# Linear attention and an expert layer on one core: another order of the instructions in chunks 2 to 8

## The chip, the cores and the metric

The kernel runs on one core of a Trainium2 chip. The metric is the device time of one execution in microseconds, lower being better. A core has engines that work side by side and wait for each other through semaphores: TensorE (PE in the rows, with PEld for its weight loads), VectorE (DVE), ScalarE (ACT), GpSimd (POOL), and SyncE (SP), which here issues the DMAs. Each engine takes its own instructions strictly in order.

## The reference

There are 8 batches of 8 heads with 576 rows of 64. The attention is linear, and its output feeds a two-layer block:

```python
q_s = exp(q - max(q, over the 64)); q_s /= sum + 1e-9
k_s = exp(k - max(k, over the 576 rows)); k_s /= sum + 1e-9
kv  = einsum('bhsd,bhse->bhde', k_s, v)        # 64 x 64 per head
x   = einsum('bhsd,bhde->bhse', q_s, kv)       # heads side by side: 4608 x 512
h   = x @ w_in                                 # 512 -> 2048
out = (h - tanh(h)) @ w_out                    # 2048 -> 512
```

## The kernel before

The 4608 rows of x go in nine chunks of 512. Chunks 0 to 7 are 512 rows of batches 0 to 7; the last 64 rows of all eight batches make chunk 8. The hidden layer goes in 16 blocks of 128 for each chunk. A matrix is held as a high part and a low part, and a product is made as three products of parts.

For each block n of a chunk the steps are these (functions in `h_parts`, lines 654 to 717, and `o_mm`, line 730). `pha`, `phb`, `phc` are four matmuls each into one PSUM tile `ph`. On ScalarE `u`, `t`, `m` (the tile mk) read `ph`, and `vv` reads u. On VectorE `g` and `tt` read `ph` and one tile in SBUF; `gg` and `cp` read SBUF alone. `gh` (ScalarE) and `gl` are the high and low part of g; gl runs on GpSimd or, with a star, on VectorE. `po n.t a` are two matmuls with gh and `po n.t b` is one with gl, for each of four row blocks t, summed over the 16 blocks. PSUM has two tiles `ph`, so `pha` of block n waits until all readers of block n-2 are done; gh, gl, g, t and u have two buffers each, mk and vv one. The second layer lags the first by two blocks.

While a chunk j is in this loop, the words with a + prepare chunk j+1. For q, in two halves 0 and 1: load `q`, maximum `mq`, subtraction `qu`, exponential `qe`, sum `sq`, scaling `qn`, transpose `tb` and a way through DRAM `qp`, `qg`. For k: load `k`, maximum `km` and on to the row of maxima `mrow` (through DRAM: `kp`, `kg`), then for the two full tiles 0 and 1 and for the remainder of 64 rows (tile `kr`, number 2) the subtraction `ks`, the exponential `ke` and the products with v, `pk`. `vo` sets the ones beside v (MEMSET on GpSimd) before `v` is loaded; v has one buffer, so `vo.1` waits for the matmuls `pk.0`. `px` makes x, `xh` and `xl` are its parts. k and v are prepared for chunks 0 to 7 alone: while chunk 7 runs, chunk 8's q is prepared and no k, and while chunk 8 runs, nothing is.

The order on every engine is written out by hand as text: FIRST (lines 32 to 101) for chunks 0 and 1, ROUND (lines 103 to 129) repeated for chunks 2 to 8, LAST for the last blocks. `run` (line 909) calls the word's function, and each engine gets its instructions in the order of the words. `go` (line 890) sends `qu`, `qn`, `gl`, `ks` to GpSimd unless the word ends with a star, which sends it to VectorE.

Of the kernel before, what the change touches and what calls it, by code (L numbers as in the profile page):

```python
# [100 lines left out]
"""  # L101

ROUND = """
ph0 po14.0a u0 po14.0b po14.1a m0 +q.0 pha1 phb1 +vo.2 +mq.0 po14.3a po15.0a po14.1b po14.3b phc1
po14.2a vv0 po14.2b t0 t1 g0 po15.2a gg0 po15.0b tt0 po15.2b cp0 u1 +vo.0 +qu.0 pha2 g1 gh0
po15.1a po15.3a phb2 +qe.0 tt1 po15.1b phc2 pha3 oc.2 po0.0a m1 oc.0 vv1 +sq.0 gg1 po15.3b u2 t2
cp1 phb3 tt2 gl0 os.2 po0.0b po0.2a po0.1a phc3 oc.3 gh1 po1.0a m2 vv2 oc.1 po0.2b g2 t3 u3 m3 gl1
po1.2a gg2 cp2 os.1 tt3 pha4 po0.3a phb4 phc4 +sa.0 os.3 +sr.0 os.0 +qn.0 vv3 po0.1b gh2 pha5 g3
po0.3b po1.1a +k.2 +tb.0 t4 gl2 po1.3a gg3 po1.0b +k.0 cp3 po1.2b u4 tt4 vv4 po2.0a po1.1b g4 gh3
po1.3b m4 po2.0b +k.1 +again +km.a po2.3a phb5 gl3* phc5 po3.0a +km.b gg4 pha6 po2.3b cp4 u5 t5  # L110
phb6 po3.3a +km.c m5 vv5 g5 +qn.1 po2.1a tt5 po3.3b +km.d po2.2a gg5 po2.2b phc6 pha7 phb7 po2.1b
cp5 gh4 po3.0b po3.1a po3.2a t6 gl4 po3.2b +qp.0 +tb.1 +kb po4.0a u6 vv6 +kr m6 +kq.1 gh5 po4.2a
phc7 po4.0b +q.1 gl5 +kq.3 po4.2b +kq.2 po5.0a po3.1b po4.3a po5.2a pha8 tt6 u7 +qp.1 g6 t7 po4.1a
gg6 +kx vv7 +kt po4.1b po5.2b po5.1a m7 phb8 phc8 cp6 +vo.1 g7 po4.3b gg7 tt7 t8 po5.3a +kp po5.0b
po5.3b po5.1b +mq.1 +v.2 +qu.1* gh6 u8 cp7 +v.0 pha9 m8 po6.0a +qg.1 phb9 gl6* gh7 tt8 g8 +kg
+ks.0* po6.1a vv8 phc9 u9 t9 gg8 +qe.1 gl7* po6.0b po7.0a po6.3a +sq.1 tt9 po6.2a +ke.0 +v.1
po6.3b po6.2b cp8 pha10 phb10 vv9 phc10 gh8 po6.1b u10 po7.3a g9 po7.0b po7.1a +sa.1 t10 po7.3b
po8.0a m9 po7.2a +pk.0 +sr.1 pha11 po7.2b po8.3a phb11 vv10 po7.1b gg9 phc11 +qn.3* cp9 +ks.2
po8.2a gl8* po8.0b pha12 phb12 m10 t11 g10 po8.1a +qn.2 +tb.3 gg10 gh9 +ks.1 gl9 u11 po9.0a phc12
po8.1b tt10 +ke.1 +qg.0 +ke.2 +pk.1 vv11 tt11 m11 u12 cp10 +pk.2 t12 po8.3b pha13 g11 po9.3a  # L120
po8.2b po9.0b gg11 cp11 +sl gh10 m12 gl10 +rs phb13 po10.0a +qp.3 +rc +tb.2 po9.2a phc13 vv12
po9.1a u13 po9.2b +qp.2 po9.1b g12 gh11 m13 tt12 +kn vv13 po9.3b po10.0b gg12 t13 po10.3a cp12
+qg.2 po10.1a po10.3b gl11 po10.2a gh12 pha14 po11.0a +px.0 +xh.0.0 g13 po10.2b +qg.3 po10.1b
phb14 gg13 tt13 +xh.0.1 phc14 po11.2a ph15 po11.2b po11.3a gl12 u14 vv14 +xl.0.0 cp13 +xl.0.1
po11.1a g14 po11.1b t14 m14 u15 po11.3b po11.0b po12.0a t15 gg14 po12.0b +px.1 po12.1a po12.2a
po12.3a gh13 tt14 cp14 tt15 gl13* po12.1b po12.3b vv15 po12.2b +xh.1.0 +sv po13.0a g15 po13.2a m15
po13.3a gh14 gg15 +xl.1.0 cp15 +xh.1.1 po13.0b gl14* po13.3b po13.2b po13.1a gh15 po13.1b +xl.1.1
gl15*
"""

LAST = """
# [841 lines left out]
```

## Time and profile before

| | us |
|---|---|
| median of 3 runs | 880.32 (880.26 to 880.8) |
| the profiled execution, its own time | 880.32 |
| its span | 878.5 |
| PE busy | 847.1 (96%) |
| DVE busy | 659.7 (75%) |
| ACT busy | 540.9 (62%) |
| POOL busy | 206.9 (24%) |

The share of busy time says which engine the span is made of; which wait costs time is seen only from the idle time of that engine, by stretch, and from what ended it. In the chain that ended last PE has 83% of the span and DVE 9%. The granted clock (PEclk) is 9 tenths or more in all 40 slices.

### The profile page before, as it was taken

The page shows a single profiled execution, that of the slowest core. Times are in us where ns is not written, and L with a number is a line of the kernel's source. Part 1 is how long each engine was busy: PE and PEld are TensorE (multiplying, and loading weights), DVE is VectorE, ACT ScalarE, POOL GpSimd, SP SyncE. Part 2 cuts the span into 40 slices and gives each one's busy share as a digit, 9 for nine tenths or more (in the row PEclk, how much of TensorE's full clock was granted, in tenths as well). Part 3 has the DMA queues.
Part 4 walks back from the last instruction along what each step waited for, and adds up shares of the span by engine and source line. Part 5 has one row for each costly group of instructions (what it writes and reads, how often), then busy time and mean ns, then how long its engine had stood idle before and what let it go on. Part 6 is the DMA issues. An engine that isn't in the chain of part 4 may idle for free.

```text
span 878.5 us, 13026 instructions
## 1 busy us (share of the span) xinstructions
PE 847.1 (96%) x4810; PEld 693.3 (79%) x4810; DVE 659.7 (75%) x1011; ACT 540.9 (62%) x955; POOL 206.9 (24%) x182
## 2 busy tenths in 40 slices
PE   2999999999999999999999999999999999999997
PEld 2888888878887888878887888788877888888885
DVE  7999989886788658866787668875796667755554
ACT  4999998565655556555665565655555565556553
POOL 4634122221312122221213121212222121201120
PEclk9999999999999999999999999999999999999999
DMA  9975301233331204320332133120422022101002
GB/s 309 362 231 205 109 1 37 84 105 89 113 91 49 67 13 138 79 71 20 115 90 72 43 115 90 49 67 37 124 69 84 20 98 58 47 4 49 1 0 49
DMA packets 103199, 75.83 MB, mean 86 GB/s; under 512 B 17376, under 2 KB 91104, under 8 KB 103136
## 3 DMA queue, kind: packets, MB, share of 16 engines
q1 hardware_dynamic: 103136, 75.01, 27.6%
q8 instruction: 38, 0.62, 0.3%
q14 instruction: 25, 0.20, 0.1%
HBM read 56.10 MB, written 18.89 MB: 85 GB/s over the span
## 4 chain that ended last, share of the span: by engine, by line
PE 83%; DVE 9%; ACT 4%; DMA 1%; issue 1%; SPq 0%; ACTq 0%
PE po L738 39%; PE ph L674 39%; DVE g L687 3%; PE px L631 2%; PE pk L417 1%; DVE t L684 1%; ACT mk L664 1%; DVE g L692 1%; DVE sq L518 1%; ACT t L664 1%; DVE g L679 1%; ACT u L664 1%; DMA k<-in_k_dram 1%; ACT q L513 1%; ACT gh L695 1%
## 5 line engine op out<-in xcount | busy, mean ns | idle before, releaser
L738 PE MATMUL po<-w_o,gh 128*128 128x512 f32 x1152 | 327.7, 391 | 0.0
L674 PE MATMUL ph<-xh,w_i 128*128 128x512 f32 x1152 | 307.0, 391 | 7.5 <-DVE t L684 7.5
L674 PEld LDWEIGHTS ph<-xh,w_i 128*128 128x128 f32 x1152 | 214.9, 188 | 55.3 <-DVE t L684 10.3
L738 PEld LDWEIGHTS po<-w_o,gh 128*128 128x128 f32 x1152 | 215.3, 188 | 45.9 <-issue 1.0
L699 POOL TENSOR_TENSOR gl<-g,gh 128x512 fp32r<-128x512 f32 x80 | 107.0, 1337 | 395.3 <-PE po L738 170.6
L738 PE MATMUL po<-w_o,gl 128*128 128x512 f32 x576 | 194.2, 392 | 0.0
L679 DVE SCALAR_TENSOR_TENSOR g<-u,ph 128x512 f32<-128x512 f32 x144 | 98.3, 683 | 100.2 <-POOL gl L699 35.4
L664 ACT ACTIVATE u<-ph 128x512 f32<-128x512 f32 x144 | 86.1, 598 | 111.5 <-PE ph L674 111.4
L674 PE MATMUL ph<-xl,w_i 128*128 128x512 f32 x576 | 154.2, 389 | 0.0
L664 ACT ACTIVATE t<-ph 128x512 f32<-128x512 f32 x144 | 85.8, 596 | 92.1 <-PE ph L674 91.7
L687 DVE SCALAR_TENSOR_TENSOR g<-vv,g 128x512 f32<-128x512 f32 x144 | 119.8, 832 | 10.5 <-ACT vv L664 6.2
L674 PEld LDWEIGHTS ph<-xl,w_i 128*128 128x128 f32 x576 | 108.1, 188 | 22.9
L738 PEld LDWEIGHTS po<-w_o,gl 128*128 128x128 f32 x576 | 107.6, 188 | 23.5 <-issue 1.2
L695 ACT CAST gh<-g 128x512 fp32r<-128x512 f32 x144 | 89.4, 621 | 59.6 <-PE po L738 43.9
L692 DVE COPY_PREDICATED g<-mk,t 128x512 f32<-128x512 int32 x144 | 120.2, 835 | 7.1 <-ACT mk L664 2.9
L684 DVE TENSOR_TENSOR t<-ph,t 128x512 f32<-128x512 f32 x144 | 98.3, 685 | 33.8 <-ACT mk L664 19.2
L664 ACT ACTIVATE vv<-u,b_pa 128x512 f32<-128x512 f32 x144 | 104.4, 725 | 6.4 <-DVE g L687 3.9
L664 ACT ACTIVATE mk<-ph 128x512 int32<-128x512 f32 x144 | 86.1, 598 | 21.4 <-DVE g L692 9.4
L699 DVE TENSOR_TENSOR gl<-g,gh 128x512 fp32r<-128x512 f32 x64 | 44.6, 697 | 20.7 <-ACT gh L695 17.1
L510 POOL TENSOR_TENSOR q<-q,mq 128x1024 f32<-128x1024 f32 x9 | 18.3, 2032 | 63.8 <-DVE mq L505 63.7
L650 ACT CAST xh<-px 128x512 fp32r<-128x512 f32 x36 | 20.4, 593 | 18.5 <-PE px L631 18.5
L652 DVE TENSOR_TENSOR xl<-px,xh 128x512 fp32r<-128x512 f32 x36 | 24.4, 686 | 7.7 <-ACT xh L650 7.1
(107 smaller groups left out, 529.6 us busy)
## 6 DMA issues: line engine op xcount, KB each, us to landing
k<-in_k_dram SPq DMA_DIRECT2D x16, 512.0 KB, 5.5
raw_i<-in_moe_w_in_dram SPq DMA_DIRECT2D x16, 512.0 KB, 7.0
raw_o<-in_moe_w_out_dram SPq DMA_DIRECT2D x16, 512.0 KB, 7.3
q<-in_q_dram SPq DMA_DIRECT2D x15, 512.0 KB, 4.3
v<-in_v_dram SPq DMA_DIRECT2D x14, 512.0 KB, 4.7
qd<-tb SPq DMA_DIRECT2D x28, 256.0 KB, 2.3
qs<-qd SPq DMA_DIRECT2D x112, 64.0 KB, 2.0
out_dram<-o SPq DMA_DIRECT2D x28, 256.0 KB, 2.2
```

Of the source, the lines that this page charges most:

```text
L510: eng.tensor_tensor(qf, qf, mq, op=ALU.subtract)
L650: nc.scalar.copy(xh, px_of[i][g])
L652: nc.vector.tensor_tensor(xl, px_of[i][g], xh.bitcast(F32), op=ALU.subtract)
L664: nc.scalar.activation(new(tag, **of), st[src], fn, **kw)
L674: nc.tensor.matmul(st["ph"], w[:, i, c], xs[j][x][:, c, :], start=n == 0, stop=n == 3 * NC - 1)
L679: nc.vector.scalar_tensor_tensor(new("g"), st["u"], C2, st["ph"], op0=ALU.mult, op1=ALU.mult)
L684: nc.vector.tensor_tensor(st["t"], st["ph"], st["t"], op=ALU.subtract)
L687: nc.vector.scalar_tensor_tensor(st["g"], st["vv"], PB, st["g"], op0=ALU.add, op1=ALU.mult)
L692: nc.vector.copy_predicated(st["g"], st["mk"], st["t"])
L695: nc.scalar.copy(new("gh", F32R), st["g"])
L699: eng.tensor_tensor(new("gl", F32R), st["g"], st["gh"].bitcast(F32), op=ALU.subtract)
L738: nc.tensor.matmul(po[key], gs[j, f][g][:, cols], wt["o", f][:, w], start=n == 1, stop=n == last)
```

## The change

Only the text ROUND is replaced; FIRST, LAST and all functions are the same. Every instruction of chunks 2 to 8 is still there, but at other places, and some change the engine. In the old text the subtractions of the keys are `+ks.0*`, `+ks.2` and `+ks.1`, in the new one `+ks.0*`, `+ks.1*` and `+ks.2*`. `+qu.1*` becomes `+qu.1`; `+qn.3*` becomes `+qn.3*` and `+qn.2*`; gl has a star in blocks 2, 3, 4, 7, 9, 13, 14, 15 where it had one in 3, 6, 7, 8, 13, 14, 15.

```diff
-+ks.0* po6.1a vv8 phc9 u9 t9 gg8 +qe.1 gl7* po6.0b po7.0a po6.3a +sq.1 tt9 po6.2a +ke.0 +v.1
...
-po8.0a m9 po7.2a +pk.0 +sr.1 pha11 po7.2b po8.3a phb11 vv10 po7.1b gg9 phc11 +qn.3* cp9 +ks.2
...
+gl8 +qu.1 u10 m10 po7.1b vv10 pha11 cp9 +qg.1 +ks.1* +ks.2* phb11 po7.2b po7.3b t10 tt10 +qe.1
```

GpSimd in chunk 4's round, which prepares chunk 5, from the second MEMSET of v on. In the names the first number is the chunk and the second the block or tile; k5_1 is the second full tile of chunk 5's keys, kr5 their remainder. Before:

```order
L298 MEMSET v5_1_4536 128x8x2
L403 TENSOR_TENSOR kr5_4346<-kr5_4346,mrow5_4586 64x512
L530 TENSOR_TENSOR q5_1_4486<-q5_1_4486,sq5_1_4610 128x8x64
L403 TENSOR_TENSOR k5_1_4379<-k5_1_4379,mrow5_4586 128x1024
L699 TENSOR_TENSOR gl4_9_4728<-g4_9_4642,gh4_9_4725 128x512
```

And now, from gl of block 6 on:

```order
L699 TENSOR_TENSOR gl4_6_4576<-g4_6_4450,gh4_6_4517 128x512
L298 MEMSET v5_1_4579 128x8x2
L301 MEMSET vr5_4615 64x8
L699 TENSOR_TENSOR gl4_8_4664<-g4_8_4563,gh4_8_4592 128x512
L510 TENSOR_TENSOR q5_1_4417<-q5_1_4417,mq5_1_4565 128x1024
L699 TENSOR_TENSOR gl4_10_4825<-g4_10_4703,gh4_10_4790 128x512
```

Both subtractions of keys (L403) are gone from GpSimd, and so is the scaling (L530) between them. Behind the MEMSET that waits for pk.0 there stand now gl of block 8 and the subtraction of q's second half (L510).

VectorE at the same place of chunk 4's round, around block 10. Before:

```order
L530 TENSOR_TENSOR q5_1_4486<-q5_1_4486,sq5_1_4610 128x8x64
L692 COPY_PREDICATED g4_9_4642<-mk4_9_4653,t4_9_4599 128x512
L699 TENSOR_TENSOR gl4_8_4700<-g4_8_4584,gh4_8_4635 128x512
L679 SCALAR_TENSOR_TENSOR g4_10_4716<-u4_10_4638,ph4_10_4620 128x512
L541 STREAM_TRANSPOSE tb23_4721<-q5_1_4486 128x256 x2
L687 SCALAR_TENSOR_TENSOR g4_10_4716<-vv4_10_4687,g4_10_4716 128x512
L684 TENSOR_TENSOR t4_10_4648<-ph4_10_4620,t4_10_4648 128x512
L684 TENSOR_TENSOR t4_11_4714<-ph4_11_4675,t4_11_4714 128x512
```

And now, from gg of block 9 on:

```order
L687 SCALAR_TENSOR_TENSOR g4_9_4619<-vv4_9_4607,g4_9_4619 128x512
L692 COPY_PREDICATED g4_9_4619<-mk4_9_4623,t4_9_4572 128x512
L403 TENSOR_TENSOR k5_1_4413<-k5_1_4413,mrow5_4585 128x1024
L403 TENSOR_TENSOR kr5_4334<-kr5_4334,mrow5_4585 64x512
L684 TENSOR_TENSOR t4_10_4693<-ph4_10_4596,t4_10_4693 128x512
L679 SCALAR_TENSOR_TENSOR g4_10_4703<-u4_10_4667,ph4_10_4596 128x512
L518 TENSOR_REDUCE sq5_1_4705<-q5_1_4417 128x16
L699 TENSOR_TENSOR gl4_9_4717<-g4_9_4619,gh4_9_4713 128x512
L687 SCALAR_TENSOR_TENSOR g4_10_4703<-vv4_10_4672,g4_10_4703 128x512
```

The two subtractions stand now behind cp of block 9 (L692) and ahead of tt (L684) and g (L679) of block 10; gg of block 10 (L687) comes three places after g where it stood two places after it, and the readers of `ph` of block 10 stand ahead of it.

## Rows read from the trace of the kernel before

**Rows 1.** Busy time by stretch: chunk 4 and chunk 7; columns as named.

```profile
core 0: us, PE busy (x) PEld busy (x) DVE busy (x) ACT busy (x) POOL busy (x), PEclk, DMA share, GB/s
...
405.63:500.28 94.65, 93.20 (x530) 75.98 (x529) 70.00 (x106) 54.35 (x97) 20.79 (x18) 1.00 0.24 74
...
689.56:782.00 92.44, 92.44 (x525) 75.97 (x524) 63.18 (x94) 52.03 (x91) 17.32 (x13) 1.00 0.17 52
```

**Rows 2.** Waits from chunk 2 on: waiter, awaited, us in total, times, longest.

```profile
PE ph L674 <- DVE t L684: 7.2, 5, 1.4
```

**Rows 3.** Timeline of PE in chunk 4: start, duration (us), engine, instruction, idle.

```profile
462.84 1.15 PE L417 MATMUL pk<-v,k 128*64 128x65 f32 x32
...
466.80 1.07 PE L674 MATMUL ph<-xh,w_i 128*128 128x512 f32 x4
467.70 0.61 PE L738 MATMUL po<-w_o,gh 128*128 128x512 f32 x2
...
469.99 1.20 PE L674 MATMUL ph<-xh,w_i 128*128 128x512 f32 x4 [1.45 <-DVE t L684]
471.02 1.08 PE L674 MATMUL ph<-xl,w_i 128*128 128x512 f32 x4
```

**Rows 4.** Timeline of DVE, the same stretch.

```profile
463.89 0.69 DVE L679 SCALAR_TENSOR_TENSOR g<-u,ph 128x512 f32<-128x512 f32 x1
...
465.18 4.15 DVE L687 SCALAR_TENSOR_TENSOR g<-vv,g 128x512 f32<-128x512 f32 x1
469.26 1.27 DVE L684 TENSOR_TENSOR t<-ph,t 128x512 f32<-128x512 f32 x2
```

**Rows 5.** Timeline of POOL, the same stretch.

```profile
464.07 0.12 POOL L298 MEMSET v<- 128x16 f32 x1 [16.96 <-PE pk L417]
464.13 1.30 POOL L403 TENSOR_TENSOR kr<-kr,mrow 64x512 f32<-64x512 f32 x1
465.39 1.04 POOL L530 TENSOR_TENSOR q<-q,sq 128x512 f32<-128x512 f32 x1
466.40 2.38 POOL L403 TENSOR_TENSOR k<-k,mrow 128x1024 f32<-128x1024 f32 x1
```

**Rows 6.** Timeline of POOL and DVE in the first part.

```profile
170.95 1.29 POOL L699 TENSOR_TENSOR gl<-g,gh 128x512 fp32r<-128x512 f32 x1 [3.43 <-ACT gh L695]
...
171.15 1.64 DVE L687 SCALAR_TENSOR_TENSOR g<-vv,g 128x512 f32<-128x512 f32 x1
...
172.19 2.36 POOL L510 TENSOR_TENSOR q<-q,mq 128x1024 f32<-128x1024 f32 x1
```

**Rows 7.** Timeline of PE and ACT at the end of chunk 3.

```profile
404.95 0.61 PE L738 MATMUL po<-w_o,gh 128*128 128x512 f32 x2
...
405.60 0.62 ACT L695 CAST gh<-g 128x512 fp32r<-128x512 f32 x1 [2.04 <-PE po L738]
```

**Rows 8.** Timeline of ACT in chunk 3.

```profile
351.06 0.72 ACT L664 ACTIVATE vv<-u,b_pa 128x512 f32<-128x512 f32 x1
351.69 0.58 ACT L664 ACTIVATE mk<-ph 128x512 int32<-128x512 f32 x1
...
358.16 0.61 ACT L695 CAST gh<-g 128x512 fp32r<-128x512 f32 x1
358.67 0.72 ACT L664 ACTIVATE vv<-u,b_pa 128x512 f32<-128x512 f32 x1
...
362.98 1.06 ACT L406 ACTIVATE k<-k 128x1024 f32<-128x1024 f32 x1
363.92 0.72 ACT L664 ACTIVATE vv<-u,b_pa 128x512 f32<-128x512 f32 x1
```

**Rows 9.** Timeline of DVE in chunk 3.

```profile
356.82 0.75 DVE L692 COPY_PREDICATED g<-mk,t 128x512 f32<-128x512 int32 x1
357.47 0.67 DVE L699 TENSOR_TENSOR gl<-g,gh 128x512 fp32r<-128x512 f32 x1
...
359.50 1.22 DVE L403 TENSOR_TENSOR k<-k,mrow 128x1024 f32<-128x1024 f32 x1
360.63 0.69 DVE L687 SCALAR_TENSOR_TENSOR g<-vv,g 128x512 f32<-128x512 f32 x1
```

More of the change, by code (lines that the diff above doesn't have):

```diff
@@ L103 @@
 ROUND = """
[L104 to L114, printed above, removed]
@@ L115 @@
-po5.3b po5.1b +mq.1 +v.2 +qu.1* gh6 u8 cp7 +v.0 pha9 m8 po6.0a +qg.1 phb9 gl6* gh7 tt8 g8 +kg
-+ks.0* po6.1a vv8 phc9 u9 t9 gg8 +qe.1 gl7* po6.0b po7.0a po6.3a +sq.1 tt9 po6.2a +ke.0 +v.1
-po6.3b po6.2b cp8 pha10 phb10 vv9 phc10 gh8 po6.1b u10 po7.3a g9 po7.0b po7.1a +sa.1 t10 po7.3b
-po8.0a m9 po7.2a +pk.0 +sr.1 pha11 po7.2b po8.3a phb11 vv10 po7.1b gg9 phc11 +qn.3* cp9 +ks.2
-po8.2a gl8* po8.0b pha12 phb12 m10 t11 g10 po8.1a +qn.2 +tb.3 gg10 gh9 +ks.1 gl9 u11 po9.0a phc12
-po8.1b tt10 +ke.1 +qg.0 +ke.2 +pk.1 vv11 tt11 m11 u12 cp10 +pk.2 t12 po8.3b pha13 g11 po9.3a
@@ L121 @@
[L121 to L126, printed above, removed]
@@ L127 @@
-po13.3a gh14 gg15 +xl.1.0 cp15 +xh.1.1 po13.0b gl14* po13.3b po13.2b po13.1a gh15 po13.1b +xl.1.1
-gl15*
+pha0 +q.0 phb0 phc0 po14.0a po14.3a u0 t0 g0 po14.0b po15.0a pha1 phb1 vv0 phc1 +mq.0 po14.2a m0
+t1 pha2 po15.0b po14.3b gg0 po15.3a u1 po14.1a po14.2b m1 tt0 po15.2a po15.3b cp0 gh0 tt1 +qu.0
+po14.1b gl0 po15.2b vv1 +vo.0 phb2 phc2 oc.0 oc.2 pha3 po0.0a g1 +qe.0 po15.1a po15.1b gg1 u2 phb3
+m2 cp1 phc3 gh1 po0.1a t2 po0.2a oc.1 oc.3 po0.0b vv2 po0.3a po1.0a pha4 u3 po0.2b tt2 po1.2a gl1
@@ new lines @@
+po1.2b phb4 m3 t3 phc4 vv3 os.0 po0.1b t4 g2 po1.0b gg2 pha5 cp2 po1.1a +k.2 gh2 po1.1b po0.3b
+po1.3a phb5 po2.0a +sq.0 os.3 +sa.0 u4 +sr.0 g3 po1.3b tt3 phc5 po2.2a os.1 gg3 os.2 vv4 cp3 gl2*
+pha6 gh3 m4 po2.3a u5 po2.1a phb6 vv5 t5 po2.1b tt4 g4 phc6 gg4 +k.0 cp4 gl3* m5 po2.0b +k.1
++again gh4 +q.1 po2.2b g5 pha7 u6 tt5 t6 vv6 gg5 cp5 po3.0a po2.3b tt6 phb7 +km.a po3.0b +qn.1
+gl4* g6 phc7 po3.2a u7 po4.0a po4.0b +km.b m6 +qn.0 po3.1a t7 gh5 +km.c gg6 po3.3a cp6 po3.1b
+po3.2b po3.3b +km.d +kb pha8 po4.3a +tb.1 po4.2a phb8 g7 po4.1a phc8 po4.3b +tb.0 m7 +v.0 +kr gh6
@@ new lines @@
+t8 po4.1b +kq.1 po4.2b tt7 po5.0a +kq.2 u8 +kq.3 +kx +qp.0 tt8 pha9 gl5 po5.0b vv7 +kt gg7 phb9
+phc9 po5.1a po6.0a m8 po5.1b cp7 g8 +mq.1 po5.2a +kp vv8 t9 po5.3a gl6 gg8 +vo.1 +qp.1 po6.0b cp8
+po5.3b +kg u9 po5.2b gh7 gh8 po6.1a pha10 tt9 po6.2a po6.1b gl7* vv9 +ks.0* +ke.0 phb10 +vo.2
+po7.0a g9 po6.3a m9 po7.0b po6.3b phc10 po6.2b po7.2a po8.0a po7.1a po7.3a +qg.0 gg9 +v.1 +pk.0
+gl8 +qu.1 u10 m10 po7.1b vv10 pha11 cp9 +qg.1 +ks.1* +ks.2* phb11 po7.2b po7.3b t10 tt10 +qe.1
+phc11 po8.1a g10 +sq.1 pha12 +v.2 gh9 po8.2a gl9* phb12 po8.0b u11 gg10 po9.0a +sa.1 +ke.1 t11
@@ new lines @@
+phc12 +sr.1 +ke.2 +qn.3* cp10 tt11 po8.3a +pk.1 +pk.2 po8.3b vv11 g11 po8.1b +qn.2* t12 po9.3a
+po8.2b +sl u12 po9.0b m11 po9.3b gg11 tt12 gh10 +rs +rc po9.2a g12 pha13 vv12 +kn phb13 +tb.3
+po9.1a phc13 po9.2b cp11 po10.0a po9.1b gl10 +px.0 gh11 m12 po10.2a po10.0b gg12 po10.1a +tb.2 u13
++xh.0.0 pha14 po10.3a po11.0a t13 tt13 gl11 phb14 cp12 +qp.3 phc14 +qp.2 po10.1b po10.2b vv13
+po10.3b gh12 g13 m13 +xh.0.1 gl12 pha15 po11.3a po11.1a t14 gg13 phb15 po11.2a phc15 po11.0b
+po11.2b cp13 +xl.0.0 u14 po11.1b po11.3b po12.0a m14 g14 tt14 po12.2a +qg.3 vv14 po12.1a po12.3a
@@ L129 @@
++qg.2 gh13 gg14 po12.1b +px.1 po12.0b +xl.0.1 u15 m15 t15 cp14 po12.3b +sv po12.2b vv15 po13.0a
+gl13* gh14 g15 gg15 +xh.1.1 po13.1a +xh.1.0 po13.2a tt15 cp15 gh15 gl14* +xl.1.0 po13.0b po13.3a
+po13.1b +xl.1.1 po13.3b gl15* po13.2b
 """
```

## The prediction

> **What bounds the kernel now.** I read the busy times first: PE is busy for 96% of the span, so the time is TensorE's work and whatever idle time lies in it. Then I cut the span at the chunks, because the text that is replaced runs once a chunk, from chunk 2 to chunk 8. A chunk with key work takes 94.65 us, of which PE is busy 93.20, while chunk 7, whose successor has no keys, has PE busy without a break [rows 1]. The list of waits says the same: from chunk 2 on PE waits for one thing only, the `tt` that frees a PSUM tile `ph`, five times, 7.2 us in all [rows 2]. So this part has 7.2 us of idle PE and no more; the rest of the idle time is in the start and the tail, which keep their order.
>
> The timeline shows the one place. `pha` of block 12 starts at 469.99 after 1.45 us of nothing, released by VectorE [rows 3]. On VectorE one `gg`, which takes 0.69 us elsewhere [rows 9], lasts from 465.18 to 469.33, and the `tt` behind it, which reads `ph` of block 10, starts at 469.26 [rows 4]. GpSimd runs three instructions without a gap over just that time, the subtraction on the remainder of the keys (kr), a scaling of q and the subtraction on a full tile (k), the last until 468.78 [rows 5]. gg waits for all three and ends 0.55 us after the last. It is no semaphore: gg had already started.
>
> That the wait is for GpSimd's use of SBUF is also seen in the first part: gg starts at 171.15 while `gl` runs on GpSimd until 172.24, and ends at 172.79, again 0.55 us later. But there it came in between gl and the q behind it, which for that ended only at 174.55 [rows 6]. So VectorE can be let in between two GpSimd instructions, and at the five stalls it was not. What differs is that the row of three begins with an instruction on 64 partitions. Why that matters no row shows.
>
> The Trainium skill (SBUF — State Buffer, section "Who interferes with whom") says that a VectorE instruction with two SBUF inputs contends with a GpSimd instruction that reads SBUF, and that the first of them has the shared pair of ports for its whole instruction. The trace agrees at 172.24 and does not at 465.4: by the rule gg would have ended near 466.0, and it ended at 469.33.
>
> **The change part by part.** *What goes.* kr, k and the scaling leave GpSimd, so gg of block 10 has nothing of that row to wait for. Each stall cost 1.45 us, and the first four matmuls after it took 1.03 us (469.99 to 471.02) where four take 0.90 (466.80 to 467.70) [rows 3], so 0.12 us more. Five times 1.57 is 7.85 us. If no new wait takes its place, the profiled execution of 880.32 us (its span is 878.5, the median of the runs is the same 880.32) becomes 872.5.
>
> *What VectorE gets.* Per chunk: the full tile's subtraction, 1.13 us from start to start [rows 9], the remainder, one more gl and one more scaling, each near the 0.6 that separates two tt [rows 4]; it loses the subtraction of q, taken at 1.13 as of the same size. The sum is about +1.8 us. VectorE was busy 70.0 of 94.65 us [rows 1], 3.46 of it the wait in gg, so it stays near 68.4 and its total decides nothing; its place in the order does.
>
> *The critical place.* Let E be the end of the last matmul with gh of block 6 (`po6.3a`), which `gh8` waits for, having one of two buffers. From there, in the new order:
> ScalarE and VectorE: gh8 starts at 0.20 (405.40 to 405.60 [rows 7]), vv9 0.51 later, the exponential ke.0 0.63 later, m9 0.94 later and 0.58 long [rows 8]; then cp9 at +0.03, ks.1 at +0.65 and ks.2 at +1.13 [rows 9]. ks.2 starts at E + 4.67.
> GpSimd: it stands at the MEMSET of v, which waits for pk.0, as it did before for 16.96 us [rows 5]. Up to pk.0 PE has 15 matmuls (po7.0b, po6.3b, phc10, po6.2b and four a-pairs) of 0.227, 3.40 us, 0.09 to the change of kind, and 1.23 from pk's start to the MEMSET (462.84 [rows 3] to 464.07 [rows 5]); two MEMSETs at 0.06 put gl8 at E + 4.84.
> PE: after pk.0 (1.17 with its edges) come 17 matmuls and then `pha` of block 12, at about E + 8.5. It needs g10, which now stands behind ks.2 and tt10 and also needs gl8, since g has two buffers.
>
> If ks.2 is first, by 0.17 us, gl8 waits for it to end near 5.34, runs its 1.29 [rows 6] to 6.63, g10 goes from 6.66 to 7.35 and PE could start at 7.39: 1.1 us to spare. This is my forecast. If gl8 is first and VectorE is let in behind it, as in rows 6, ks.2 ends at 6.13 + 0.55, tt10 starts at 6.59, g10 0.59 later and ends at 7.87: still in time. Only a GpSimd row that lets nobody in costs anything (first rival).
>
> *The other edges.* `qu.1` on GpSimd runs behind gl8 until about 8.5, and ScalarE's queue stands at qe.1 until then, with gh9, u11, ke.1 and t11 behind it. The first of them that PE wants is gh9, at `po9.0a`, 11 us after E; qe.1 and gh9 take 1.6 us, so it comes near 10.2. The tightest edge that I found elsewhere is `pha` of block 6: from the end of po1.3a PE has 13 matmuls, 2.95 us, and the chain gh3 0.20, m4 0.51 and 0.58, tt4 0.03, g4 0.59 and 0.69, and 0.04 to PE is 2.64: 0.3 us to spare. The transfers keep their size, and each lands microseconds ahead of its reader by the same counting, so I take nothing for them; without that cover a late one is the third rival.
>
> **The rivals.**
> First, the same stall from another row: gl8 is first and qu.1 follows with no opening. qu.1 takes between 1.76 us (from gg's end to its own) and 2.36 [rows 6]; with 1.9, near the lower, GpSimd is done at 8.03, ks.2 ends at 8.58, g10 at 9.77, PE starts at 9.81: 1.3 us late, 1.43 with the refill, 7.2 us in five chunks, 879.7. For it: the margin is 0.17 us, and a MEMSET on 64 partitions stands right ahead of gl8. Against it: ks.2 is the earlier, and rows 6 show an opening. By the skill's rule this rival would cost nothing.
>
> Second, small new gaps: an edge like block 6 misses. With 0.3 us and the refill of 0.12 in each of seven chunks that is 2.9 us, 875.4. For it: a margin of 0.3 on a chain of seven rows. Against it: both ends hang on the same matmul, so they shift together.
>
> Third, slower: ks.1 too is caught behind gl8 and qu.1. It starts at E + 3.54, so cp9 has to be 1.3 us later; it waits for m9 behind ke.0, which needs ks.0, and this the row of maxima from DRAM. I place the end of ks.0 at E - 0.2 and ke.0 at E + 1.34, so from 2.8 us of delay on it is caught. Then ks.1 ends near 9.1, tt10 starts at 9.6, g10 ends at 10.9, PE is 2.45 us late, 2.57 with the refill, 12.9 us in five chunks: 885.4. For it: ks.0 stands just behind a transfer through DRAM and back. Against it: the 2.8 us.
>
> **How the numbers follow.** No new stall, 872.5: 0.62. Small gaps, 873 to 878 about 875.4: 0.17. The same stall, 879.7: 0.11. Slower, 885.4 or something that I have not seen: 0.10. A measurement of this kernel tells about 0.2%, 1.8 us, from no change. The first two are faster, 0.79; the third case is within that bound, 0.11; slower 0.10. The low end is 871.8, the forecast less a tenth more for each stall; the high end takes in the small gaps and stops short of the third case, 879: some 0.2 is left out.
>
> **What would show it.** Right: in the profile after, PE has no idle time from chunk 2 on, a chunk with keys takes 93.1 us, no gg lasts over 2 us, GpSimd waits for pk.0 some 13 us and then runs gl and q, and the two key subtractions on VectorE (L403) last about 1.2 and 0.65. The first rival would show as a L403 of 64 partitions lasting over 3 us and PE idle before block 12 again; the second as PE idle of tenths in all seven chunks; the third as a late L403 of a full tile. My forecast is wrong if PE waits at any place by more than 0.5 us per chunk.

## The result, and the profile after

The changed kernel takes 871.69 us, median of 4 runs (871.5 to 871.78); the kernel before, in the same comparison, 880.34 us (880.26 to 880.8). The ratio is 0.99, its 95% interval 0.9883 to 0.9918: 8.65 us faster. The forecast was 872.5 us with a range from 871.8 to 879, so the time lies 0.8 us under the forecast and 0.1 us under the range's low end.

The profiled execution took 871.78 us, its span is 869.7. The same two stretches as in [rows 1], each from the first `pha` of its chunk; the second ends 2.7 us inside chunk 8, as that of [rows 1] does by 2.5 us (columns: length of the stretch, then busy time and count of each engine, granted clock, DMA):

```profile
core 0: us, PE busy (x) PEld busy (x) DVE busy (x) ACT busy (x) POOL busy (x), PEclk, DMA share, GB/s
402.24:495.17 92.93, 92.93 (x530) 76.07 (x528) 69.39 (x109) 54.46 (x97) 18.13 (x15) 1.00 0.26 76
681.03:773.50 92.47, 92.47 (x526) 76.21 (x525) 63.88 (x95) 51.62 (x91) 18.17 (x12) 1.00 0.16 52
```

Chunk 4 is 92.93 us long instead of 94.65, and PE is busy for all of it; chunk 7, up to the first `pha` of chunk 8, takes 89.74 us where it took 89.90. The difference in chunk 4, 1.72 us, comes five times: from the first `pha` of chunk 2 to that of chunk 7 it is 464.65 us instead of 473.21, 8.56 less, nearly the whole gain. VectorE stands at 69.39 us: `gg` gives back 3.5 us, and `copy_predicated` (the step `cp`) takes 14.8 us for its 16 instructions instead of 12.8, three of which now last 1.5 to 1.75 us beside an instruction of GpSimd, at places where PE does not come to wait for them.

The list of PE's waits has the line of [rows 2] no more; what is left (what waited, what it waited for, us in total, times, longest) lies in the first part, before 216 us. Two of its lines:

```profile
PE pm L332 <- DVE km L326: 12.4, 1, 12.4
...
PE ph L674 <- DVE t L684: 0.3, 1, 0.3
```

The critical place in chunk 4, GpSimd first:

```profile
460.48 0.12 POOL L298 MEMSET v<- 128x16 f32 x1 [13.10 <-PE pk L417]
460.52 0.10 POOL L301 MEMSET vr<- 64x8 f32 x1
460.58 1.75 POOL L699 TENSOR_TENSOR gl<-g,gh 128x512 fp32r<-128x512 f32 x1
462.29 1.91 POOL L510 TENSOR_TENSOR q<-q,mq 128x1024 f32<-128x1024 f32 x1
```

and VectorE beside it:

```profile
459.37 1.21 DVE L403 TENSOR_TENSOR k<-k,mrow 128x1024 f32<-128x1024 f32 x1
460.50 0.67 DVE L403 TENSOR_TENSOR kr<-kr,mrow 64x512 f32<-64x512 f32 x1
461.24 0.69 DVE L684 TENSOR_TENSOR t<-ph,t 128x512 f32<-128x512 f32 x1
462.37 0.69 DVE L679 SCALAR_TENSOR_TENSOR g<-u,ph 128x512 f32<-128x512 f32 x1 [0.44 <-POOL gl L699]
```

GpSimd waits 13.10 us for `pk.0`, as foreseen, and its `gl` comes 0.08 us after the remainder's subtraction (64 partitions, L403) has begun on VectorE. So `gl` is the one that waits, and ends at 462.33; `g` of block 10 follows 0.04 us later, and PE, which needs it for `pha` of block 12, never stops.

### The profile page after: what moved, and what is told of

The parts are those of the page before. It is cut to its first block, busy times and chain, and to the rows that moved or that the text cites. A ratio compares the mean times of both kernels' runs of the same rounds, so it can differ in the third digit from the quotient of the medians.

```text
span 869.7 us, 13011 instructions
## 1 busy us (share of the span) xinstructions
PE 846.1 (97%) x4810; PEld 693.9 (80%) x4810; DVE 656.3 (75%) x1028; ACT 541.2 (62%) x955; POOL 193.7 (22%) x165
## 4 chain that ended last, share of the span: by engine, by line
PE 93%; DVE 3%; DMA 2%; ACT 1%; issue 0%; POOL 0%; ACTq 0%; DVEq 0%
PE po L738 45%; PE ph L674 44%; PE px L631 2%; PE pk L417 2%; DMA k<-in_k_dram 1%; DMA q<-in_q_dram 1%; DVE mq L505 0%; PE pb L391 0%; DVE g L687 0%; DVE k L403 0%; DVE xl L652 0%; DVE g L692 0%; ACT q L513 0%; POOL q L510 0%; PE pt L584 0%
## 5 line engine op out<-in xcount | busy, mean ns | idle before, releaser
L738 PE MATMUL po<-w_o,gh 128*128 128x512 f32 x1152 | 324.4, 391 | 0.0
L699 POOL TENSOR_TENSOR gl<-g,gh 128x512 fp32r<-128x512 f32 x73 | 102.1, 1399 | 422.7 <-PE po L738 225.1
L738 PE MATMUL po<-w_o,gl 128*128 128x512 f32 x576 | 190.5, 393 | 0.0
L679 DVE SCALAR_TENSOR_TENSOR g<-u,ph 128x512 f32<-128x512 f32 x144 | 97.8, 679 | 60.3 <-POOL gl L699 25.7
L692 DVE COPY_PREDICATED g<-mk,t 128x512 f32<-128x512 int32 x144 | 131.1, 910 | 10.7 <-ACT mk L664 6.6
L684 DVE TENSOR_TENSOR t<-ph,t 128x512 f32<-128x512 f32 x144 | 98.5, 684 | 49.2 <-ACT t L664 27.9
L687 DVE SCALAR_TENSOR_TENSOR g<-vv,g 128x512 f32<-128x512 f32 x144 | 103.4, 718 | 18.0 <-ACT vv L664 15.1
L699 DVE TENSOR_TENSOR gl<-g,gh 128x512 fp32r<-128x512 f32 x71 | 49.4, 695 | 22.7 <-PE po L738 22.0
L510 POOL TENSOR_TENSOR q<-q,mq 128x1024 f32<-128x1024 f32 x14 | 29.4, 2099 | 73.0 <-DVE mq L505 72.9
L518 DVE TENSOR_REDUCE sq<-q 128x16 f32<-128x1024 f32 x15 | 18.2, 1211 | 11.9 <-ACT q L513 11.9
L513 ACT ACTIVATE q<-q 128x1024 f32<-128x1024 f32 x15 | 15.9, 1060 | 17.0 <-POOL q L510 17.0
```

What stands on the lines that cost most here:

```text
L510: eng.tensor_tensor(qf, qf, mq, op=ALU.subtract)
L518: nc.vector.tensor_reduce(sq, qf, axis=AX.X, op=ALU.add)
L679: nc.vector.scalar_tensor_tensor(new("g"), st["u"], C2, st["ph"], op0=ALU.mult, op1=ALU.mult)
L684: nc.vector.tensor_tensor(st["t"], st["ph"], st["t"], op=ALU.subtract)
L687: nc.vector.scalar_tensor_tensor(st["g"], st["vv"], PB, st["g"], op0=ALU.add, op1=ALU.mult)
L692: nc.vector.copy_predicated(st["g"], st["mk"], st["t"])
```

## The experiments

Two questions stood open: why gg of block 10 was held over three GpSimd instructions before the change [rows 4, 5], and which part of the change sets it free. Here a row is a run of GpSimd instructions without a gap, an opening is the moment between two of them at which VectorE can be let in, and the height of an instruction is the number of its partitions. Theory A said that a row, once it begins with an instruction on fewer than 128 partitions, lets no VectorE instruction with two inputs in SBUF in until the row ends; B, that any row does so; C, that only the new order as a whole helps; D, that the remainder costs wherever it stands on GpSimd. Every run below is of the whole kernel. Each except the two on other heights was timed against the kernel before on the same chip: 880.48 us for the first four, 880.42 us for the next four.

| run | GpSimd's row, partitions | gg of block 10 held until | us | ratio, interval |
|---|---|---|---|---|
| before | 64, 128, 128 | end of the row | 880.34 | |
| remainder on VectorE | 128, 128 | let in before the second | 871.78 | 0.9901 (0.9886–0.9916) |
| multiplication, 128 | 128, 128, 128 | end of the second | 871.96 | 0.9901 (0.9886–0.9916) |
| swapped | 128, 128, 64, 128 | end of the first | 871.68 | 0.9899 (0.9884–0.9914) |
| new order, remainder back | 128, 128, 64 | nothing came in that row | 871.46 | 0.9898 (0.9882–0.9915) |
| multiplication, 64 | 64, 128, 128 | end of the row | 879.57 | 0.9988 (0.9979–0.9998) |
| new order, remainder late | 128, 128 | the remainder's subtraction came there, not gg: end of the first | 871.74 | 0.9902 (0.9887–0.9916) |
| tt10 first | 64, 128, 128 | end of the row | 871.61 | 0.9898 (0.9884–0.9913) |
| tt10 first, remainder second | 128, 64, 128 | end of the row | 871.63 | 0.9898 (0.9882–0.9915) |
| multiplication, 96 | 96, 128, 128 | end of the row | 879.30, one run | |
| multiplication, 32 | 32, 128, 128 | end of the row | 879.19, one run | |

**The remainder on VectorE, all else in the old order.** In the text of the round `+ks.2` goes from behind cp9 to behind tt10, with the star that means VectorE:

```diff
-... phc11 +qn.3* cp9 +ks.2
+... phc11 +qn.3* cp9
-po8.1b tt10 +ke.1 +qg.0 +ke.2 +pk.1 ...
+po8.1b tt10 +ke.1 +qg.0 +ks.2* +ke.2 +pk.1 ...
```

> The old order; only the subtraction on the remainder of the keys goes from GpSimd to VectorE (behind tt of block 10), so GpSimd's row behind the MEMSET is the scaling of q and then the full tile. Theory A (GpSimd's row shuts VectorE out between its instructions because it begins with one on 64 partitions): gg of block 10 comes at about 465.2, just after the full tile's subtraction has started, waits for that one and ends near 468.1 where it ended at 469.3; of the 1.7 us that a stall costs about 0.4 stay, five times: 874. Theory B (any row of GpSimd instructions without a gap shuts VectorE out to the row's end): the same, since the row ends with the same instruction. Theory C (the assignment does not matter, only the new order): about 880.

Measured 871.78 us: all of the gain, with one instruction moved. GpSimd and VectorE in chunk 4:

```profile
460.72 1.05 POOL L530 TENSOR_TENSOR q<-q,sq 128x512 f32<-128x512 f32 x1
461.73 2.85 POOL L403 TENSOR_TENSOR k<-k,mrow 128x1024 f32<-128x1024 f32 x1
```

```profile
461.64 0.67 DVE L687 SCALAR_TENSOR_TENSOR g<-vv,g 128x512 f32<-128x512 f32 x1
```

gg began 0.13 us before the scaling of q ended, had its usual 0.67 us, and it was GpSimd's full tile, ready at 461.73, that waited (2.85 us instead of the 2.38 of [rows 5]). The time expected was some 2 us too long: gg came a little earlier than it was put, in time for the opening. C falls. A stands: the row has full height throughout, and gg was let in at the opening. B does not fit, since the full tile follows the scaling without a gap; but gg came so near to the opening that the next run puts B to a plainer test.

**The same, with a full row.** At the remainder's old place GpSimd multiplies one half of a key tile by ones (`one` is a tile of ones), on 128 partitions, which changes no value. The row has three instructions as before but begins with full height. Against the first run:

```diff
-... phc11 +qn.3* cp9
+... phc11 +qn.3* cp9 +kz
+            call["kz"] = lambda: nc.gpsimd.tensor_tensor(
+                st["k", 1][:, :, 0], st["k", 1][:, :, 0],
+                one.unsqueeze(2).broadcast_to([P, H, D]), op=ALU.mult,
+            )
```

> As the run before, but at the old place of the remainder's subtraction GpSimd multiplies half of the full tile by ones on all 128 partitions (values unchanged), so that the row has three instructions again, about 1.04, 1.04 and 2.4 us, none on 64 partitions. Theory A: gg of block 10 comes during the second and is let in before the third, ends near 466.7, and no stall is left: 871.7. Theory B: gg ends behind the third, near 469.1, and the stall stays: 879 to 880.

871.96 us. GpSimd's row and gg:

```profile
459.99 1.04 POOL L850 TENSOR_TENSOR k<-k,one 128x512 f32<-128x512 f32 x1
460.99 1.05 POOL L530 TENSOR_TENSOR q<-q,sq 128x512 f32<-128x512 f32 x1
462.00 2.84 POOL L403 TENSOR_TENSOR k<-k,mrow 128x1024 f32<-128x1024 f32 x1
```

```profile
461.03 1.55 DVE L687 SCALAR_TENSOR_TENSOR g<-vv,g 128x512 f32<-128x512 f32 x1
```

The row has three instructions without a gap, and gg came in between the second and the third: it ends at 462.58, 0.54 us after the second. B falls.

**The two subtractions change places**, `+ks.1` behind cp9 and `+ks.2` behind gh9, both still on GpSimd:

```diff
-... phc11 +qn.3* cp9 +ks.2
+... phc11 +qn.3* cp9 +ks.1
-... +qn.2 +tb.3 gg10 gh9 +ks.1 gl9 ...
+... +qn.2 +tb.3 gg10 gh9 +ks.2 gl9 ...
```

> The old order and the old engines; only the words of the full tile's and the remainder's subtraction change places, so GpSimd runs the full tile first (2.4 us), then the scaling, then the 64 partitions. Theory A: gg of block 10 comes during the first, is let in at its end near 466.5, ends near 467.1, and no stall is left: 871.7, though not one instruction has changed its engine. Theory B: gg waits for the whole row and ends near 469.3: 880.3.

871.68 us. No instruction changed its engine, and the gain is whole:

```profile
460.65 2.40 POOL L403 TENSOR_TENSOR k<-k,mrow 128x1024 f32<-128x1024 f32 x1
463.00 1.50 POOL L530 TENSOR_TENSOR q<-q,sq 128x512 f32<-128x512 f32 x1
464.47 1.29 POOL L403 TENSOR_TENSOR kr<-kr,mrow 64x512 f32<-64x512 f32 x1
```

```profile
461.66 1.93 DVE L687 SCALAR_TENSOR_TENSOR g<-vv,g 128x512 f32<-128x512 f32 x1
```

gg came in behind the first (463.05 to its end at 463.59). The remainder stands third here, with gl right behind it:

```profile
465.72 1.30 POOL L699 TENSOR_TENSOR gl<-g,gh 128x512 fp32r<-128x512 f32 x1
```

No VectorE instruction with two inputs in SBUF came between its start and the start of gl, so this run does not try the opening behind it. It does show that the remainder on GpSimd need not cost anything, which D denies.

**The new order, with the remainder back on GpSimd**, behind gl8 and qu.1:

```diff
-... cp9 +qg.1 +ks.1* +ks.2* phb11 ...
+... cp9 +qg.1 +ks.1* +ks.2 phb11 ...
```

> The new order, with the remainder's subtraction alone put back on GpSimd, where it stands behind gl of block 8 and the subtraction of q's second half. Theory A: no VectorE instruction with two SBUF inputs comes in that time, so nothing is shut out, and the time is that of the new kernel, 871.7 within 0.5. Theory D (64 partitions on GpSimd cost their stall wherever they stand): 879 to 880.

871.46 us, so D falls. The remainder on GpSimd, and what VectorE runs from gl8 to its end:

```profile
463.62 1.29 POOL L403 TENSOR_TENSOR kr<-kr,mrow 64x512 f32<-64x512 f32 x1
```

```profile
461.15 0.69 DVE L684 TENSOR_TENSOR t<-ph,t 128x512 f32<-128x512 f32 x1 [0.66 <-ACT t L664]
461.82 0.69 DVE L679 SCALAR_TENSOR_TENSOR g<-u,ph 128x512 f32<-128x512 f32 x1
464.78 1.22 DVE L518 TENSOR_REDUCE sq<-q 128x16 f32<-128x1024 f32 x1 [2.27 <-ACT q L513]
```

None of these has two inputs in SBUF. In the new order it is not the remainder's move to VectorE that pays but the place where it stands.

Three theories were left for the hold: A as it stands (A1); A2, that the height of the instruction beside which gg comes decides, since before the change gg came during the remainder [rows 4, 5]; and F, that the subtraction itself does it, by its tile or its operands.

**The multiplication on 64 partitions.** The second run again, with one thing different, the height:

```diff
-                st["k", 1][:, :, 0], st["k", 1][:, :, 0],
-                one.unsqueeze(2).broadcast_to([P, H, D]), op=ALU.mult,
+                st["k", 1][:REST, :, 0], st["k", 1][:REST, :, 0],
+                one[:REST].unsqueeze(2).broadcast_to([REST, H, D]), op=ALU.mult,
```

> The old order with the remainder's subtraction on VectorE, and at its old place on GpSimd a multiplication by ones on 64 partitions of a key tile. It differs from the run with the multiplication on 128 partitions (871.96 us) in that height alone; both add an instruction that changes nothing. A1 (a GpSimd row that begins with 64 partitions keeps gg out of every opening until the row ends): gg of block 10 comes as before the change, lasts over 3 us and ends 0.55 us after the full tile's subtraction, PE waits some 1.5 us before block 12 in five chunks, 879 to 881 us. A2 (gg is kept out if a 64-partition instruction runs at the moment when it comes): gg came at the multiplication's last 0.01 us in the run on 128 partitions, so the stall if it comes a little earlier here, none if it comes a little later. F (not the height, but the subtraction itself, its tile or its row of maxima): gg is let in behind the multiplication or the scaling, within 2 us, 871.5 to 872.3 us.

879.57 us. The stall is back. GpSimd, VectorE, and PE's wait:

```profile
464.43 1.04 POOL L850 TENSOR_TENSOR k<-k,one 64x512 f32<-64x512 f32 x1
465.43 1.04 POOL L530 TENSOR_TENSOR q<-q,sq 128x512 f32<-128x512 f32 x1
466.44 2.38 POOL L403 TENSOR_TENSOR k<-k,mrow 128x1024 f32<-128x1024 f32 x1
```

```profile
465.49 3.88 DVE L687 SCALAR_TENSOR_TENSOR g<-vv,g 128x512 f32<-128x512 f32 x1
469.29 0.68 DVE L684 TENSOR_TENSOR t<-ph,t 128x512 f32<-128x512 f32 x1
```

```profile
PE ph L674 <- DVE t L684: 6.3, 6, 1.3
```

Five of these six waits, 6.0 us, lie from chunk 2 on.
The first two instructions on GpSimd take what they took at full height. gg came 0.02 us after the lower one, when the second, on 128 partitions, had begun, and was let in neither behind that nor before 469.37, 0.55 us after the row. In chunk 2 gg came during the lower instruction itself, 0.09 us before its end, and was held as well:

```profile
275.62 1.03 POOL L850 TENSOR_TENSOR k<-k,one 64x512 f32<-64x512 f32 x1
```

```profile
276.56 4.01 DVE L687 SCALAR_TENSOR_TENSOR g<-vv,g 128x512 f32<-128x512 f32 x1
```

At 128 partitions gg of chunk 2 came as near to the end, 0.12 us before it, and took 0.66 us. So the height does it, and neither the tile, the operation nor the number of instructions in the row (F falls). Chunk 4 speaks against A2 as well, but 0.02 us is little.

**The first rival of the forecast, made to happen.** In the new order a copy of the remainder onto itself delays its subtraction until gl8 runs on GpSimd:

```diff
-... cp9 +qg.1 +ks.1* +ks.2* phb11 ...
+... cp9 +qg.1 +ks.1* +kc +ks.2* phb11 ...
+            call["kc"] = lambda: nc.vector.tensor_copy(st["k", NKP], st["k", NKP])
```

> The new order with a copy of the remainder onto itself on VectorE between the two key subtractions (0.6 us a chunk, changes nothing), so that the remainder's subtraction comes about 0.5 us after GpSimd's gl8 has begun, ahead of qu.1, behind two MEMSETs of which the second is on 64 partitions. This makes the first rival of the forecast happen. If the MEMSET on 64 partitions counts as the beginning of the row: the subtraction is kept out through qu.1 until about 464.2 us of chunk 4, g10 ends near 465.5, PE waits about 1.2 us before block 12 in five chunks, 877 to 880 us. If only the height of the instructions that read SBUF counts (A1, A2): it is let in behind gl8, at about 461.8, ends near 462.4, tt10 and g10 end near 463.7, PE waits for nothing, 871.5 to 872.3 us. The copy alone costs nothing, since VectorE is idle for some 0.4 us there and for 2.3 us behind g10.

871.74 us. GpSimd and VectorE:

```profile
460.54 0.11 POOL L301 MEMSET vr<- 64x8 f32 x1
460.60 1.48 POOL L699 TENSOR_TENSOR gl<-g,gh 128x512 fp32r<-128x512 f32 x1
462.05 2.35 POOL L510 TENSOR_TENSOR q<-q,mq 128x1024 f32<-128x1024 f32 x1
```

```profile
460.96 1.67 DVE L403 TENSOR_TENSOR kr<-kr,mrow 64x512 f32<-64x512 f32 x1
...
463.15 0.67 DVE L679 SCALAR_TENSOR_TENSOR g<-u,ph 128x512 f32<-128x512 f32 x1
```

The subtraction came 0.36 us after gl8 and was let in behind it: it ends at 462.63, and gl8 at 462.08. The MEMSET on 64 partitions right ahead of gl8 closed nothing. The margin of 0.17 us on which the forecast's first rival hung decides nothing: lost, it costs PE nothing.

**One word moved in the kernel before**, tt10 ahead of gg10:

```diff
-... g10 po8.1a +qn.2 +tb.3 gg10 gh9 ...
-po8.1b tt10 +ke.1 ...
+... g10 po8.1a +qn.2 +tb.3 tt10 gg10 gh9 ...
+po8.1b +ke.1 ...
```

> The kernel before with one word moved: tt10 stands ahead of gg10 on VectorE, everything stays on its engine. tt10 reads one tile of SBUF and frees ph, so PE should not wait before block 12 even if gg10 is held: 871.5 to 872.3 us by all of the theories on GpSimd's row; the rival is that g10, cp10 and what follows come so late behind the held gg10 that PE waits elsewhere, 875 to 880 us. The trace tells A1 from A2: gg10 now comes some 0.6 us later, when the remainder's subtraction (64 partitions, first of the row) is over or nearly so and the scaling of q runs. A1: it is held until 0.55 us after the full tile's subtraction all the same, over 3 us. A2: it is let in behind the scaling, 1 to 1.5 us.

871.61 us. GpSimd's row is that of before, and so is the hold:

```profile
460.70 1.30 POOL L403 TENSOR_TENSOR kr<-kr,mrow 64x512 f32<-64x512 f32 x1
461.97 1.05 POOL L530 TENSOR_TENSOR q<-q,sq 128x512 f32<-128x512 f32 x1
462.98 2.40 POOL L403 TENSOR_TENSOR k<-k,mrow 128x1024 f32<-128x1024 f32 x1
```

```profile
461.75 0.65 DVE L684 TENSOR_TENSOR t<-ph,t 128x512 f32<-128x512 f32 x1
462.33 3.60 DVE L687 SCALAR_TENSOR_TENSOR g<-vv,g 128x512 f32<-128x512 f32 x1
```

gg is held for 3.60 us, until 0.55 us after the row, and PE does not wait: tt10, which frees `ph`, went by at 461.75 while the remainder's subtraction ran, in its usual time; it has one input in SBUF. What cost the time was never the hold as such but that tt10 stood behind it. It came 0.33 us after the remainder had ended, during the scaling, and was not let in behind that: A2 falls.

**The same, and the remainder second in the row**, behind the scaling of q:

```diff
-... phc11 +qn.3* cp9 +ks.2
-... +qn.2 +tb.3 tt10 gg10 gh9 ...
+... phc11 +qn.3* cp9
+... +qn.2 +ks.2 +tb.3 tt10 gg10 gh9 ...
```

> As the run before (tt10 ahead of gg10), and the remainder's subtraction moved on GpSimd behind the scaling of q: the row is scaling (128 partitions), remainder (64), full tile (128). gg10 comes about 1.6 us after the row's beginning, while the remainder's subtraction runs. A1 (the first instruction of the row decides): it is let in behind the remainder's subtraction, 1 to 1.5 us long. A2 (the instruction that runs when gg comes decides): it is held until 0.55 us after the full tile's subtraction, over 3 us. The time is 871.5 to 872.3 us by both, as tt10 does not wait.

```profile
460.82 1.05 POOL L530 TENSOR_TENSOR q<-q,sq 128x512 f32<-128x512 f32 x1
461.83 1.28 POOL L403 TENSOR_TENSOR kr<-kr,mrow 64x512 f32<-64x512 f32 x1
463.07 2.39 POOL L403 TENSOR_TENSOR k<-k,mrow 128x1024 f32<-128x1024 f32 x1
```

```profile
462.32 3.69 DVE L687 SCALAR_TENSOR_TENSOR g<-vv,g 128x512 f32<-128x512 f32 x1
```

The row begins on 128 partitions and gg, which came during the remainder, is still held until 0.55 us after the last. So A was too narrow: the instruction on fewer partitions need not stand first. What holds wherever gg was held is that from the lower instruction on, to the end of these rows of three, the openings are shut. The time, 871.63 us, is again free of the hold.

**Other heights**, the multiplication with `96` and `32` in place of `REST` (which is 64), one run each:

> As the run with the multiplication by ones on 64 partitions (879.57 us, gg of block 10 held 3.88 us), but on 96 partitions. If any instruction on fewer than 128 partitions closes the rest of GpSimd's row: gg over 3 us in five chunks, about 879.6 us. If it takes half the partitions or fewer: gg is let in behind the scaling of q, some 1.5 us, about 871.9 us, as with 128.

> As the run before, on 32 partitions. If fewer than 128 partitions close the row, or half and fewer: gg over 3 us, about 879.6 us. If it is 64 alone that does it: some 1.5 us and about 871.9 us.

First 96 partitions, then 32:

```profile
463.78 1.04 POOL L850 TENSOR_TENSOR k<-k,one 96x512 f32<-96x512 f32 x1
```

```profile
464.82 3.90 DVE L687 SCALAR_TENSOR_TENSOR g<-vv,g 128x512 f32<-128x512 f32 x1
```

```profile
463.65 1.03 POOL L850 TENSOR_TENSOR k<-k,one 32x512 f32<-32x512 f32 x1
```

```profile
464.70 3.90 DVE L687 SCALAR_TENSOR_TENSOR g<-vv,g 128x512 f32<-128x512 f32 x1
```

gg lasts 3.90 us in both, and the times are 879.30 and 879.19 us. It is not half the height but less than the whole that shuts the row.

No version was faster than the changed kernel by more than the spread of the runs. In it, as in every run near 871.7 us, the list of PE's waits is empty from chunk 2 on, so no wait of PE is left there for another order to remove; those that are left stand in the first part, which all of them share.

## What the prediction had right, and the step that failed

*The bound and its cause.* The forecast took all of the gain from one stall, five times. That held, and only its size was off: 5 times 1.72 us is 8.6 of the 8.65 measured, and the run with tt10 first gets the same from that one wait alone.

*The step that failed* is "Each stall cost 1.45 us, and the first four matmuls after it took 1.03 us … so 0.12 us more. Five times 1.57 is 7.85 us." The 1.45 is the idle time that the timeline prints, and that is counted from a matmul's modelled end, 0.39 us after its start, while the next one normally starts 0.23 us after it (four in 0.90 in [rows 3]). The row of the kernel before that shows it is the last one ahead of the stall:

```profile
468.16 0.39 PE L738 MATMUL po<-w_o,gl 128*128 128x512 f32 x1
```

From its start to the next, 469.99, are 1.83 us; less the 0.23 that it would have taken anyway, the stall is 1.60 us, and with the 0.12 after it 1.72, just what a chunk became shorter by. Five times 0.15 is nearly all of the 0.8 us by which the forecast was too long; the low end, "a tenth more for each stall", 0.7 below it, was 0.1 short. No reason was given for that tenth. The refill of 0.12 was right.

*The mechanism.* "What differs is that the row of three begins with an instruction on 64 partitions. Why that matters no row shows" was the right difference, as the runs with 64 and with 128 partitions show, though "begins" was too narrow. The change removed the row as a whole, and so would have paid under each of the theories A to D: its time alone does not tell them apart, the runs do. Why it matters no run shows either.

*The critical place* came as worked out: gl8 0.08 us behind the remainder where 0.17 was given, GpSimd's wait 13.10 us, the subtractions 1.21 and 0.67 us. *VectorE's total* was given as 68.4 and is 69.39 us; the held `copy_predicated`, which add 2.0 us to their group's durations, were not in the sum, and cost PE nothing.

*The rivals.* Small new gaps did not come: the edge at block 6 with its 0.3 us held. The first rival was priced at 879.7 us for lost margin; the run with the late remainder lost it and stayed at 871.74, since the opening of a row of full height was there. The third never came near.

## What to carry to other kernels

Count a stall of a pipelined engine from start to start, less the usual pitch, not by the idle time of a timeline that knows only modelled ends. When an instruction lasts several times its usual length without a semaphore, look at what GpSimd (or, for GpSimd, VectorE) reads from SBUF beside it, and first ask whether what stands behind it in its queue could go ahead: here one word moved was worth as much as the whole new order. Put what runs on fewer than 128 partitions late in a row of GpSimd, where no VectorE instruction with two inputs in SBUF comes behind it, or on VectorE.

## What the runs showed of the hardware

- An instruction of GpSimd that reads SBUF on 32, 64 or 96 partitions shut the openings between it and those that followed without a gap: in chunk 4 gg lasted 3.60 to 4.15 us and ended 0.54 to 0.56 us after the last of them, in six kernels of six. No row had more than two instructions behind the lower one with a VectorE instruction waiting, and why the height does this no run shows. Where all that read SBUF ahead of the opening had 128 partitions, the waiting VectorE instruction (gg in two runs, the remainder's subtraction in one) was let in behind the instruction beside which it came and ended 0.54 or 0.55 us after it; gg that came 0.13 us before the end took its usual 0.67 us. A MEMSET on 64 partitions, which reads nothing, shut no opening behind it.
- By the Trainium skill (SBUF — State Buffer, section "Who interferes with whom") the first of the two has the pair of ports for its whole instruction, and one that only writes SBUF does not contend. The rows of full height and the MEMSET agree; the rows with a lower instruction do not, and there the measurement decides.
- The other side pays as well: with gg let in ahead of it, GpSimd's full tile took 2.85 us instead of 2.38.
